# The last steps of the first attention group, reordered: transposes and copy of a pair of head columns, and the product of head 5

## The chip, the cores and the metric

The kernel runs on one core of a Trainium2 chip. The metric is device time in microseconds (us) of one execution; the time before is the median of five runs.

## The reference

Two operations follow one another. The first is causal attention over 4 batches, 8 heads, 768 positions and a head size of 64. Three heads (0, 2, 6) attend to all earlier positions; the other five see only the first 4 positions (sinks) and a window of the last 64. The second is a mixture of 4 experts on the 3072 x 512 attention output, all four applied to every token and weighted by normalised probabilities.

```python
scores = scale * np.matmul(q, k.transpose(0, 1, 3, 2))
causal = rel >= 0
stream_keep = causal & (is_sink | in_win)          # is_sink: key < 4; in_win: 0 <= rel < 64
mask = np.where(retr[0, :, 0, 0, None, None], full_mask, stream_mask)
...
a = a / (np.sum(a, axis=-1, keepdims=True) + 1e-09)
attn_out = np.matmul(a, v)
x = np.ascontiguousarray(attn_out.transpose(0, 2, 1, 3)).reshape(B * S, H * D)
p = domain_probs / (domain_probs.sum(-1, keepdims=True) + 1e-09)
for e in range(E):
    h = np.maximum(x @ w1[e], 0.0)
    out += p[:, e:e + 1] * (h @ w2[e])
```

## The kernel before

The 3072 tokens are cut into 8 groups of 384 (batch b, half c). Attention of a group leaves its result in a tile `xT` with the 512 model columns on partitions, as four columns of 128 that each hold two heads: `PLACE[h] = (h % 4, h // 4)`, so column 0 holds heads 0 and 4, column 1 heads 1 and 5, column 2 heads 2 and 6, column 3 heads 3 and 7. The MoE layers read `xT` as the moving operand. The first group's attention runs alone at the start, up to about 21 us; the attention of the other groups is mixed in small steps into the MoE work of earlier groups.

The order of instructions on each engine is written out by hand: an engine executes what the Python program issues for it in that order. The program is made of generators. Each `yield` hands over an estimate in ns, and the driver adds it to a running clock with `tick`. Work that should not stand too early in VectorE's queue is booked on a list, `behind`, with a due time of the clock plus `LAG` = 1300; `tick` issues from the front of the list what has come due:

```python
def later(op, g):
    behind.append((clock[0] + LAG, op, g))
def tick(ns):
    clock[0] += ns
    while behind and behind[0][0] <= clock[0]:
        behind.pop(0)[1]()
```

A retrieval head (`values_r`, L713) gives its values with tokens on partitions; the pair of heads 2 and 6 is normalised into `x_pair`, and `x_transposes(6)` turns it: three matmuls with the identity (L762) into a pV bank, and one VectorE copy (L766) into column 2 of `xT`. A streaming head (`values`, L785) has its values already turned. Its matmuls write a pO bank (heads of the upper half) or a pV bank. ScalarE takes the logarithm of the sums (L803) and the exponential of its negative (L813), and a booked `scale` multiplies on VectorE into the head's half of its `xT` column (L808). The loop over a streaming head's matmuls hands over inside only where the estimate passes 300 ns with matmuls left:

```python
ns += mm_ns(nq)
if ns > 300 and n < len(work) - 1:
    yield ns
    ns = 0
```

Here `mm_ns(cols)` is `cols / 2.4 + 2.5`. In the first group a streaming head has two score tiles with the parts 160 and 160, and 160 and 96 columns, so four value matmuls.

The first group ends with the values of heads 5 and 7 and the transposes of head 6's pair; then `tick(LAG)` and `small_things` (masks and the normalising of probabilities on VectorE). The driver's next work is `plain_steps` of expert 0. It opens four blocks of layer 1 (L1027), one PSUM bank each. For each block it issues the matmuls of columns 0, 2 and 1, block after block, and then column 3 of each, followed by the block's ReLU on ScalarE (L1040). Layer 2 is L1048. GpSimd issues the weight loads (L334, L340), and the loads of queries, keys and values.

Of the kernel before, what the change touches and what calls it, by code (L numbers as in the profile page):

```python
# [18 lines left out]
def kernel(  # L19
# [147 lines left out]
    def half(u):  # L167
        return slice(u * D, (u + 1) * D)
# [25 lines left out]
    def v_tile(b, c, h, t):  # L194

        if b:
            return v_tiles(b, c, h)[:, t, :]
        return v_tiles(b, t // TC, h)[:, t % TC, :]
# [115 lines left out]
    def sink_row(h):  # L314

        t = v_tiles(0, 0, h)
        nc.vector.tensor_copy(
            out=t[0:NS, :, own_v(h)],
            in_=v_s32[:, h : h + 1, :].to_broadcast([NS, TC, D]),
        )  # L320

    def sink_rows(b, c):
        if b:
            put_sinks(windows(vSf), v_sinks, c)
            return
        for t in range(TC):
            nc.sync.dma_start(
                out=vS[0:NS, c, t, :, :], in_=vS[R0 : R0 + NS, 0, 0, :, :]
            )
# [97 lines left out]
    def warm_up(ps, n, cols):  # L427
        for _ in range(n):
            nc.tensor.matmul(  # L429
                out=ps[:, 0:cols], lhsT=warm[:, 0:P], rhs=warm[:, 0:cols],  # L430
                start=True, stop=True,
            )
# [103 lines left out]
    def mm_ns(cols):  # L536
        return cols / 2.4 + 2.5

    def attention(b, c):
# [213 lines left out]
        def x_transposes(h):  # L753
            ct = PLACE[h][0]
            x = x_pair if ct else x_one
            r = slice(0, P) if ct else half(0)
            if h == 6:
                ps = pV.tile([P, 512], FP32, name="pV", bufs=2)
            else:
                ps = pO.tile([P, 512], FP32, name="pO", bufs=2)  # L760
            for j in range(3):
                nc.tensor.matmul(  # L762
                    out=ps[r, j * P : (j + 1) * P], lhsT=x[:, j, r], rhs=ident16,
                    start=True, stop=True,
                )
            nc.vector.tensor_copy(out=xT[g][r, ct, :], in_=ps[r, 0:CH])  # L766

        def values(h):
            if RETR[h]:
                yield from values_r(h)  # L770
                return
            ct, u = PLACE[h]
            if first and u == 1:
                ps = pO.tile([P, 512], FP32, name="pO", bufs=2)
            else:
                ps = pV.tile([P, 512], FP32, name="pV", bufs=2)
            if first:
                warm_up(ps, {3: 3, 4: 3, 5: 4, 7: 3}.get(h, 0), 256)
            work = []
            for es, parts in es_of[h]:  # L780
                for t, o, q0, nq in parts:
                    work.append((es, t, o, q0, nq))
            ns = 0
            for n, (es, t, o, q0, nq) in enumerate(work):
                nc.tensor.matmul(  # L785
                    out=ps[:, q0 : q0 + nq],
                    lhsT=v_tile(b, c, h, t),
                    rhs=es[:, o : o + nq],
                    start=(n == 0),
                    stop=(n == len(work) - 1),  # L790
                    skip_group_check=True,
# [6 lines that stand above are left out]
            r, o = half(u), half(1 - u)  # L798
            pair = first and h in (3, 4)
            if not pair or u == 0:  # L800
                rc_of[0] = att.tile([P, CH], FP32, name="rc", bufs=2)
            rc = rc_of[0]
            nc.scalar.activation(  # L803
                out=rc[r, :], in_=ps[o, 0:CH], func=AF.Ln, bias=eps[o, :]
            )

            def scale(r=r, ps=ps):
                nc.vector.tensor_tensor(  # L808
                    out=xT[g][r, ct, :], in0=ps[r, 0:CH], in1=rc[r, :], op=ALU.mult
                )  # L810

            if not pair:
                nc.scalar.activation(out=rc[r, :], in_=rc[r, :], func=AF.Exp, scale=-1.0)  # L813
                later(scale, g)
            elif u == 0:
                scale_of[0] = scale
            else:
                nc.scalar.activation(out=rc, in_=rc, func=AF.Exp, scale=-1.0)
                later(scale_of[0], g)
                later(scale, g)  # L820

            yield ns + (600.0 if g == 1 else 400.0)

        def both(a, bb):

            gens = [a, bb]
            while gens:
                for gg in list(gens):
                    try:
                        yield next(gg)  # L830
                    except StopIteration:
                        gens.remove(gg)
# [4 lines left out]
        if first:  # L837
            yield from transposes(0)
            yield from scores(0)
            sink_row(1)  # L840
            sink_row(3)
            yield from transposes(1)
            yield from scores(2)
            sink_row(4)
            sink_row(5)
            sink_row(7)
            yield from both(scores(1), values(0))
            yield from transposes(2)
            yield from both(scores(3), values(2))
            x_transposes(0)  # L850
            yield from scores(4)
            yield from transposes(3)
            yield from values(1)
            yield from both(scores(5), values(3))
            yield from both(scores(6), values(4))
            yield from both(scores(7), values(6))
            yield from values(5)
            yield from values(7)
            x_transposes(6)
            tick(LAG)  # L860
            small_things()
        else:
            order = (0, 2, 6, 1, 3, 5, 7, 4) if by_dma else (0, 2, 1, 3, 6, 5, 7, 4)
            more = divmod(g + 1, NCH) if g + 1 < G else None
            if not by_dma:
                sink_rows(b, c)

            def behind_values(h):
                if more and not RETR[h]:
                    load_v(*more, [h])  # L870
            if by_dma:
                keys_to_rows(b, c)
                yield 1500.0
            else:
                yield from transposes(0)
                yield from transposes(1)

            waiting = []
            for n, h in enumerate(order):
                v_steps, done = iter(()), None  # L880
                ahead = sum(len(score_tiles(x)) for x in (*waiting, h))
                if len(waiting) > 1 or (waiting and ahead > 6):
                    done = waiting.pop(0)
                    v_steps = values(done)
                for m, step in enumerate(both(scores(h), v_steps)):
                    yield step
                    if not by_dma and n == 1 and m == 1:
                        yield from transposes(3)
                if done is not None:
                    behind_values(done)  # L890
                waiting.append(h)
                if n < 3 and by_dma:
                    keys_to_windows(b, c, n)
                if n == 1 and by_dma:
                    sink_rows(b, c)
                if n == 3 and more and g > 1:
                    transpose_rows(*more)
                if not by_dma and n == 2:
                    yield from transposes(2)
            if more:  # L900
                if g == 1:
                    load_probs(pair0)
                    transpose_rows(*more)
            for h in waiting:
                yield from values(h)
                behind_values(h)

    def small_things():
        def to_mask(x, bias):
            nc.vector.tensor_scalar(  # L910
                out=x, in0=bias, scalar1=0.0, scalar2=None, op0=ALU.is_ge
            )

        to_mask(mC, bC)
        to_mask(mS[:, 0:3, :], bS)
        to_mask(mS[:, 3, :], bS[:, 2, :])
        normalise(probs, psums, p_sb)
# [21 lines left out]
    behind = []  # L939
# [3 lines left out]
# [7 lines that stand above are left out]
# [487 lines left out]
    for ns in attention(0, 0):  # L1437
        tick(ns)
# [108 lines left out]
```

The softmax here doesn't subtract the row's maximum and nothing guards it: scores larger than these inputs give would overflow.

## Time and profile before

| | us |
|---|---|
| median of five runs | 377.53 (377.0 to 377.95) |
| profiled execution, its own time | 377.52 |
| its span | 375.8 |
| TensorE busy | 368.1 (98%) |
| VectorE busy | 282.4 (75%) |
| ScalarE busy | 227.7 (61%) |
| granted TensorE clock | 0.999 |

The span runs from the first to the last instruction of the profiled execution; 1.7 us of its time lie outside. Engines are named PE (TensorE matmuls), PEld (its weight loads), DVE (VectorE), ACT (ScalarE), POOL (GpSimd) and SP (the sync engine). A line number such as L766 is that of the kernel. On a timeline, a row has its start, its length, engine, line, operation, what it writes and reads, the shape, the count of instructions merged into it, and in brackets how long its engine was idle before it and what released it.

### The profile page before, as it was taken

Reading aid. Unit: us, or ns where it says so; the run is one execution under the profiler, and the core shown is the slowest. Engines: PE = TensorE matmul, PEld = TensorE weight load, DVE = VectorE, ACT = ScalarE, POOL = GpSimd, SP = SyncE. Lnnn points to the kernel's source line nnn. Section 1 sums busy time; section 2 is a strip of 40 time slices with the busy share of each in tenths; the row PEclk is TensorE's granted clock in tenths of the full one; section 3 lists DMA queues with packets and bytes.
Section 4 is the critical chain, followed back from the end, with each engine's and each line's share of the span. In section 5 each row is a group of like instructions: output and inputs, shape, how many; then the busy total and the mean of one; then the engine's idle time right before and its main releaser. Section 6 shows DMA issues by size and latency. Waiting matters only on the chain.

```text
span 375.8 us, 10137 instructions
## 1 busy us (share of the span) xinstructions
PE 368.1 (98%) x4128; PEld 311.0 (83%) x4128; DVE 282.4 (75%) x620; ACT 227.7 (61%) x475; POOL 112.8 (30%) x155
## 2 busy tenths in 40 slices
PE   8889999999999999999999999999999999999996
PEld 4755466668998988999989898998899998999996
DVE  7774768697888679878758858967778868769572
ACT  3863478547785785765676955784777361450630
POOL 8933673693058038115601650320000000000000
PEclk9999999999999999999999999999999999999999
DMA  9999999999799579988904991951220300300101
GB/s 164 152 201 205 185 192 192 181 205 116 83 117 153 103 97 120 149 117 63 206 9 62 169 156 19 129 126 14 72 69 2 111 5 0 114 2 6 54 2 56
DMA packets 124771, 39.24 MB, mean 104 GB/s; under 512 B 113728, under 2 KB 118404, under 8 KB 124724
## 3 DMA queue, kind: packets, MB, share of 16 engines
q0 software_dynamic: 86848, 19.01, 58.5%
q1 hardware_dynamic: 36276, 19.18, 23.3%
q8 instruction: 32, 0.52, 0.6%
q10 hardware_dynamic: 1600, 0.39, 0.5%
q14 instruction: 15, 0.12, 0.1%
HBM read 44.89 MB, written 6.34 MB: 136 GB/s over the span
## 4 chain that ended last, share of the span: by engine, by line
PE 94%; DVE 3%; ACT 2%; issue 0%; ACTq 0%
PE pO L1290 31%; PE pA L1154 25%; PE pO L1183 9%; PE pA L1027 7%; PE pO L1048 7%; PE pA L659 5%; PE pV L713 2%; PE pV L785 2%; PE pA L1183 2%; PE pO L429 1%; PE pA L557 1%; ACT rc L803 1%; DVE xs L1112 1%; ACT es L677 1%; DVE kR L576 1%; PE pA L1380 0%
## 5 line engine op out<-in xcount | busy, mean ns | idle before, releaser
L1290 PEld LDWEIGHTS <-hA 128*128 128x128 f16 x1104 | 104.9, 98 | 12.3
L1154 PE MATMUL pA<-xs,w1sb 128*128 128x256 f16 x864 | 109.3, 272 | 0.0
L1154 PEld LDWEIGHTS <-w1sb 128*128 128x128 f16 x864 | 80.7, 98 | 8.5
L1163 ACT ACTIVATE hA<-pA 128x512 f16<-128x512 f32 x108 | 64.4, 597 | 35.2 <-PE pA L1154 32.9
L1290 PE MATMUL pO<-w2sb,hA 128*128 128x256 f16 x640 | 76.7, 272 | 0.0
L677 ACT ACTIVATE es<-pA 128x384 f16<-128x384 f32 (+2 forms) x122 | 59.2, 512 | 26.7 <-PE pA L659 22.9
L305 POOL DMA_DIRECT2D vS<-in_v_dram x30 | 29.6, 986 | 113.3 <-PE pV L785 110.1
L1290 PE MATMUL pO<-tsb,hA 128*128 128x256 f16 x464 | 56.7, 272 | 0.0
L1112 DVE TENSOR_TENSOR xs<-xT,pB 128x1024 f16<-128x1024 f16 (+1 forms) x52 | 49.5, 970 | 1.2 <-DMA xT<-x_pair 1.2
L967 DVE TENSOR_TENSOR hA<-hA 128x1024 f16<-128x1024 f16 x60 | 39.6, 684 | 0.4
L1040 ACT ACTIVATE hA<-pA 128x384 f16<-128x384 f32 (+1 forms) x64 | 22.2, 385 | 19.9 <-PE pA L1027 19.7
L1027 PE MATMUL pA<-xT,w1sb 128*128 128x384 f16 (+1 forms) x256 | 30.9, 273 | 1.3 <-DVE xT L766 0.8
L1048 PE MATMUL pO<-w2sb,hA 128*128 128x512 f16 x128 | 30.7, 379 | 0.0
L1310 ACT COPY s<-pO 128x256 f32<-128x256 f32 x31 | 11.5, 372 | 27.7 <-PE pO L1290 21.9
L1027 PEld LDWEIGHTS <-w1sb 128*128 128x128 f16 x256 | 19.3, 98 | 10.2 <-issue 1.9
L808 DVE TENSOR_TENSOR xT<-pV,rc 64x384 f16<-64x384 f32 x37 | 20.5, 555 | 9.0 <-ACT rc L813 6.6
L1183 PEld LDWEIGHTS <-w1sb 128*128 128x128 f16 x416 | 26.3, 98 | 1.1 <-issue 0.2
L803 ACT ACTIVATE rc<-pV,eps 64x384 f32<-64x384 f32 x37 | 21.3, 575 | 6.5 <-PE pV L785 5.9
L1199 DVE TENSOR_TENSOR hA<-pO,s 128x512 f16<-128x512 f32 x26 | 17.9, 687 | 9.3 <-PE pO L1183 6.7
L681 DVE TENSOR_TENSOR es<-es,mS 128x384 f16<-128x384 f16 (+1 forms) x40 | 13.7, 344 | 13.5 <-ACT es L677 13.4
L1193 ACT COPY s<-pO 128x512 f32<-128x512 f32 x39 | 22.5, 586 | 1.4 <-PE pO L1183 1.2
L1183 PE MATMUL pO<-xs,w1sb 128*128 128x128 f16 x312 | 23.3, 219 | 0.0
(144 smaller groups left out, 498.3 us busy)
## 6 DMA issues: line engine op xcount, KB each, us to landing
pB<-p_rows SPq DMA_DIRECT2D x10, 512.0 KB
out_dram<-o SPq DMA_DIRECT2D x19, 256.0 KB
w1sb<-in_moe_w_dram POOLq DMA_DIRECT2D x8, 512.0 KB, 9.2
w2sb<-in_moe_w_dram POOLq DMA_DIRECT2D x4, 1024.0 KB, 12.5
vS<-in_v_dram POOLq DMA_DIRECT2D x30, 112.0 KB, 4.2
k_rows<-in_k_dram POOLq DMA_DIRECT2D x18, 128.0 KB, 5.0
q<-in_q_dram POOLq DMA_DIRECT2D x18, 128.0 KB, 6.4
vR<-in_v_dram POOLq DMA_DIRECT2D x24, 48.0 KB, 5.7
```

The lines of the kernel that those rows point to most:

```text
L305: gp.dma_start(out=t[:, :, own_v(h)], in_=windows_of(v, b, h, c))
L677: nc.scalar.activation(out=es[:, 0:cols], in_=ps[:, 0:cols], func=AF.Exp, scale=SC)
L803: nc.scalar.activation(out=rc[r, :], in_=ps[o, 0:CH], func=AF.Ln, bias=eps[o, :])
L967: nc.vector.tensor_tensor(out=out, in0=a, in1=b, op=ALU.subtract)
L1027: nc.tensor.matmul(out=pss[ft][:, 0:cols_n], lhsT=w1sb[:, e * DMP + ct, ft * P : (ft + 1) * P], rhs=x[:, ct, :], start=(n == 0), stop=(n = ...
L1048: nc.tensor.matmul(out=ps_o, lhsT=hs[:, ft, j * P : (j + 1) * P], rhs=w2sb[:, e * FTP + ft, :], start=(ft == 0), stop=(ft == FTP - 1),)
L1112: nc.vector.tensor_tensor(out=o, in0=xin, in1=pb.to_broadcast([P, DMP, n, P]), op=ALU.mult)
L1154: nc.tensor.matmul(out=ps[:, f * PC : (f + 1) * PC], lhsT=w1sb[:, e * DMP + ct, (f0 + f) * P : (f0 + f + 1) * P], rhs=xs[:, ct, :], start= ...
L1163: nc.scalar.activation(out=blocks[:, b0 : b0 + 2, k0 : k0 + 2, :].rearrange("p t f x -> p f t x"), in_=ps.rearrange("p (f t x) -> p f t x" ...
L1183: nc.tensor.matmul(out=ps[:, f * P : (f + 1) * P], lhsT=w[:, ct, f * P : (f + 1) * P], rhs=a[:, ct, :], start=(first and f == 0 and ct == ...
L1193: nc.scalar.copy(out=kept[n], in_=ps)
L1290: nc.tensor.matmul(out=ps, lhsT=a[:, k, :], rhs=b(k), start=(first and k == 0), stop=(k == KT - 1), skip_group_check=not first,)
```

## The change

At the end of the first group, the last entry of `behind` is taken off once head 5's values have been issued; it is head 5's booked product. The generator of head 7's values is then advanced by one step, the transposes and the copy of the pair (`x_transposes(6)`) are issued, head 5's product is booked again with the clock of that moment, and the rest of head 7's generator follows. `tick(LAG)` and `small_things` come after that, as before.

```diff
             yield from both(scores(6), values(4))
             yield from both(scores(7), values(6))
             yield from values(5)
-            yield from values(7)
+            at_once = behind.pop()
+            v_steps = values(7)
+            yield next(v_steps)
             x_transposes(6)
+            later(*at_once[1:])
+            yield from v_steps
             tick(LAG)
             small_things()
```

## Prediction

> **What bounds the kernel now.** I read the page's busy times first, then the chain that ended last, then TensorE's waits after the first group, then the timelines of TensorE, VectorE and ScalarE around 20 us, where the change lies.
>
> From the page, busy time by engine and the shares of the chain:
>
> ```profile
> PE 368.1 (98%) x4128; PEld 311.0 (83%) x4128; DVE 282.4 (75%) x620; ACT 227.7 (61%) x475; POOL 112.8 (30%) x155
> PE 94%; DVE 3%; ACT 2%; issue 0%; ACTq 0%
> ```
>
> TensorE works for 368.1 of 375.8 us and is 94% of the chain. [...] its queue has hardly a hole: what delays it delays the end. Its waits after 20 us (engine and line, what it waited for: us in total, times, longest):
>
> ```profile
> PE pA L1027 <- DVE xT L766: 0.8, 1, 0.8
> PE pV L713 <- DVE es L681: 0.6, 1, 0.6
> PE pA L1027 <- DMA w1sb<-in_moe_w_dram: 0.4, 1, 0.4
> ```
>
> There are three, and two stand at the seam that the change touches, where the first MoE layer begins. The seam on the timelines (start us, us, engine, line, operation, count, idle before and its releaser); TensorE, then VectorE, then ScalarE. The last two TensorE rows are from narrow windows and share a matmul: it starts at 22.06:
>
> ```profile
> 19.66 0.41 PE L785 MATMUL pO<-es,vS 128*128 128x160 f16 x4
> 20.05 0.34 PE L762 MATMUL pV<-ident,x_pair 128*128 128x128 f16 x3
> 20.76 0.32 PE L1027 MATMUL pA<-xT,w1sb 128*128 128x384 f16 x1 [0.36 <-DMA w1sb<-in_moe_w_dram]
> 21.89 0.48 PE L1027 MATMUL pA<-xT,w1sb 128*128 128x384 f16 x2 [0.81 <-DVE xT L766]
> 22.06 0.65 PE L1027 MATMUL pA<-xT,w1sb 128*128 128x384 f16 x3
> ...
> 20.69 0.56 DVE L808 TENSOR_TENSOR xT<-pO,rc 64x384 f16<-64x384 f32 x1 [0.70 <-ACT rc L813]
> 21.28 0.56 DVE L766 CAST xT<-pV 128x384 f16<-128x384 f32 x1
> 21.87 0.56 DVE L808 TENSOR_TENSOR xT<-pO,rc 64x384 f16<-64x384 f32 x1
> 22.47 0.23 DVE L910 TENSOR_SCALAR mC<-early 128x256 f16<-128x256 f16 x1
> ...
> 19.53 0.57 ACT L803 ACTIVATE rc<-pO,eps 64x384 f32<-64x384 f32 x1 [0.30 <-PE pO L785]
> 20.14 0.52 ACT L813 ACTIVATE rc<-rc 64x384 f32<-64x384 f32 x1
> 20.68 0.57 ACT L803 ACTIVATE rc<-pO,eps 64x384 f32<-64x384 f32 x1
> 21.29 0.52 ACT L813 ACTIVATE rc<-rc 64x384 f32<-64x384 f32 x1
> ```
>
> VectorE does head 5's product (20.69), the pair's copy (21.28), head 7's product (21.87). Plain_steps takes its columns in the order 0, 2, 1, 3. Column 0 starts at 20.76; column 2, the pair, waits for the copy until 21.89; column 1, with head 5, follows at 22.06 without a wait, its product having ended at 21.25. Column 3, with head 7, is asked for only after twelve matmuls. ScalarE's reciprocal of head 7 ends at 21.29 + 0.52 = 21.81, and head 7's product can't start before it.
>
> [...] the matmuls behind column 2 of the first block, on columns ready long before, stood still until 21.89. [...] the copy's transposes ended at 20.05 + 0.34 = 20.39, yet it ran only after head 5's product. [...] Here that hop is 0.03 us from ScalarE to VectorE (20.66 to 20.69) and 0.05 from VectorE to TensorE (21.84 to 21.89).
>
> **The change, part by part.** It adds and removes no instruction and no DMA. What counts is the order in which instructions are issued.
>
> *The transposes.* Read literally, they should fall within head 7's value matmuls. They don't. The generator of head 7 hands over inside its loop only once its estimate exceeds 300 ns with matmuls left. In this group a streaming head has four matmuls of 160, 160, 160 and 96 columns; at columns / 2.4 + 2.5 they come to 69, 138, 207 and 250, so it never does. Its first yield is its last: all four matmuls, both ScalarE operations and the booking of head 7's product have been issued. TensorE's order is as before, value matmuls at 19.66 and transposes at 20.05. Cost 0, and ScalarE's order is unchanged too.
>
> *The copy.* Head 5's product has been taken off the list, so the copy is first on VectorE. It waits for the transposes, 20.39; with a hop of 0.03 it runs 20.42 to 20.98. No row shows it so early; whether 0.02 sooner or 0.5 later doesn't matter, for it isn't what ends last below. Column 2 of the first block could then start at 20.98 + 0.05 = 21.03, 0.86 us earlier.
>
> *Head 5's product.* It is booked again only after the transposes, and head 7's was booked inside the step before. The list is served from its front: at tick(LAG) **head 7's product comes out first, head 5's second**. Head 7's product waits for ScalarE until 21.81, so it starts at 21.84 and ends at 22.40. VectorE's starts in this row are 0.59 apart: head 5's product runs 22.43 to 22.99, although its inputs were there at 20.66. It has gone from first to third. VectorE stands idle from 20.98 to 21.84.
>
> *TensorE behind it.* The third matmul of the first block, column 1, needs head 5's product: 22.99 + 0.05 = 23.04, where it started at 22.06. **That is 0.98 us later.** Behind it in program order stand the other columns of that block, the next three blocks, and the whole kernel. Only one matmul, column 2's, moves in front of the wait; it was the one just ahead of column 1 before, so the displacement of everything from column 1 on is 0.98. Column 3 asks for head 7's product (22.40) ten matmuls after that and waits for nothing.
>
> *What hides nothing of it.* After this seam TensorE's waits name one stall, 0.57 us before 43.59 (L713, for a mask product on VectorE). Followed back, VectorE there runs without a hole from 40.20, when it was released by TensorE's own transposes at 39.80; it moves along. From then on the longer pieces of the chain are TensorE's, apart from two of 1.13 us on VectorE near 205, which follow earlier TensorE work. No transfer is awaited after 20.76.
>
> *What moves beside it, at no cost.* The masks and the normalising of the probabilities begin behind the third product, 23.03 for 22.47: 0.56 later, with SP's store of the probability rows (27.02) behind them and SP's four copies of sinks after that. VectorE is idle 2.12 us before its next use at 29.11 (from its timeline), and the first reader of the masks is past 43. Without that cover it would be 0.56, still less than TensorE's own shift. GpSimd's loads up to 30 us wait for earlier loads, not for this. The two pO banks are read until 22.99; TensorE next writes one past 27.
>
> *The clock.* The third matmul waits from about 21.35 to 23.04, 1.7 us; the longest hole so far was 1.03 (before 18.35), and the granted clock reads 1.00 in every slice. [...] I take 0[...].
>
> Sum: +0.98 on the profiled execution's 377.52 us (span 375.8, so 1.7 outside it) gives 378.50; the median shown, 377.53, is the same within 0.01, so **378.5 us**.
>
> **The rivals.** *Head 5's product directly behind the copy*, the reading that the words suggest. Then it runs 21.01 to 21.57, column 1 starts at 21.62, 0.44 earlier than 22.06, and head 7's product at 21.84 is in time: 377.1, not slower. It decides on one point: whether head 5's product leaves the list before head 7's. It is no loss as long as that product ends by 22.01. For it: the four value matmuls could be handed over in two pieces if the estimate passed 300. Against it: the sum is 250.
>
> *The delay is partly swallowed.* If the stall before 43.59 is held by something that doesn't move, up to 0.57 comes back: +0.41, 377.9. Against it is the chain from 39.80 just given.
>
> *The clock drops.* [...] Against it is the hole's length; for it, that only two of this layer's matmuls run between 20.4 and 23.0.
>
> *The change doesn't do what it says*: as to the transposes that holds already, and is in the main case.
>
> **How the numbers follow.** Main case 0.80, 378.5 with its own spread of 0.3; swallowed 0.08, 377.9; clock 0.06[...]; the other order 0.06, 377.1. A measurement of this kernel can tell about 0.2%, 0.75 us, from no change: slower means over 378.28. The main case lies 0.22 above that, and some 0.07 of its chance falls below; with the swallowed case and most of the other order, same is 0.15, faster 0.02, slower 0.83. The range, 377.9 to 379.2, holds the main case, half the swallowed one and a clock loss of up to 0.7; about 0.16 is left out.
>
> **What the next profile would show.** VectorE at the seam: the copy near 20.42, then an idle of about 0.85 released by ScalarE L813, then two L808 products near 21.84 and 22.43. TensorE: one L1027 at 20.76, one near 21.03, then a wait of about 1.7 us for xT of L808, and the rest from 23.04. ScalarE's four rows as they were. If one product stands between copy and 21.6, the order is the rival's. If the seam is as said and the end isn't about 1 us later, look at 43: the L713 stall would be shorter. A granted clock under 1.0 in the slices up to 30 us would be the clock's.

## The result, and the profile after

| | before | changed |
|---|---|---|
| median, us | 377.5 (41 executions) | 379.7 (22 executions) |
| lowest to highest | 377.0 to 378.53 | 377.87 to 380.52 |
| profiled execution, its span | 377.52, 375.8 | 379.7, 378.0 |
| mean granted TensorE clock there | 0.999 | 0.995 |

The ratio is 1.005, with a 95% interval of 1.0041 to 1.0059. That is slower, as forecast, but by 2.2 us where 1.0 was forecast, and above the range. The clock records fall into two groups: 15 of the 22 executions stand at 0.994 or 0.995 and took 379.38 to 380.52, the other 7 at 0.999 or 1.0 and took 377.87 to 379.31. Of these seven, five lie between 377.87 and 378.31, and two, at 379.30 and 379.31, close to the first group; they were not profiled.

The seam (the place where the first group's attention ends and the first layer begins) comes first: the timelines of the changed kernel around 20 us, TensorE, VectorE and ScalarE (start us, length us, engine, line, operation, count; idle before and its releaser in brackets). Lines behind the change are four higher: L1027 is now L1031, L1048 is L1052.

```profile
20.06 0.34 PE L762 MATMUL pV<-ident,x_pair 128*128 128x128 f16 x3
20.77 0.60 PE L1031 MATMUL pA<-xT,w1sb 128*128 128x384 f16 x2 [0.37 <-DMA w1sb<-in_moe_w_dram]
22.93 6.71 PE L1031 MATMUL pA<-xT,w1sb 128*128 128x384 f16 x30 [1.56 <-DVE xT L808]
...
20.44 0.56 DVE L766 CAST xT<-pV 128x384 f16<-128x384 f32 x1 [0.44 <-PE pV L762]
21.85 1.03 DVE L808 TENSOR_TENSOR xT<-pO,rc 64x384 f16<-64x384 f32 x2 [0.85 <-ACT rc L813]
22.91 0.23 DVE L914 TENSOR_SCALAR mC<-early 128x256 f16<-128x256 f16 x1
...
21.30 0.52 ACT L813 ACTIVATE rc<-rc 64x384 f32<-64x384 f32 x1
```

The order is the one read from the code. The transposes are where they were. The copy is first on VectorE, at 20.44. VectorE then idles 0.85 us for head 7's reciprocal, and both products follow in one row of two, head 7's and then head 5's. TensorE does two matmuls of the layer, columns 0 and 2, and stands 1.56 us for head 5's product. Column 1 starts at 22.93 for 22.06, 0.87 later.

The rest is in the same TensorE row: thirty matmuls take 6.71 us, where thirty-one took 5.45 in the kernel before:

```profile
21.89 5.45 PE L1027 MATMUL pA<-xT,w1sb 128*128 128x384 f16 x31 [0.81 <-DVE xT L766]
```

The clock row of the profile's 40 slices and the stretches after 22 us of the changed kernel show why (columns: stretch, its length, busy us and count of TensorE, its weight loads, VectorE, ScalarE and GpSimd, the granted clock, DMA share, GB/s):

```profile
PEclk9989999999999999999999999999999999999999
```

```profile
core 0: us, PE busy (x) PEld busy (x) DVE busy (x) ACT busy (x) POOL busy (x), PEclk, DMA share, GB/s
22.00:23.00 1.00, 0.07 (x1) 0.06 (x1) 0.97 (x3) 0.00 (x0) 0.43 (x1) 1.00 1.27 212
23.00:24.00 1.00, 1.00 (x6) 0.52 (x6) 0.90 (x7) 0.00 (x0) 0.00 (x0) 0.76 1.24 208
24.00:25.00 1.00, 1.00 (x5) 0.50 (x4) 0.97 (x6) 0.00 (x0) 0.00 (x0) 0.50 1.15 180
25.00:26.00 1.00, 1.00 (x5) 0.50 (x4) 0.97 (x2) 0.00 (x0) 0.00 (x0) 0.50 1.15 209
26.00:27.00 1.00, 1.00 (x5) 0.48 (x4) 0.97 (x4) 0.89 (x3) 0.30 (x2) 0.53 1.09 201
27.00:28.00 1.00, 1.00 (x8) 0.59 (x6) 0.43 (x2) 1.00 (x3) 0.77 (x1) 1.00 1.13 213
```

In the row of slices only the third, 18.9 to 28.4 us, is under 9. In the stretches the busy share is 1.00 from 23 us on and tells nothing apart; the count does: five matmuls touch a microsecond in which the clock reads 0.50, eight the one after it. From one matmul's start to the next it is 0.32 us there, and 0.16 after it. The clock reads 0.50 from 23.52 (0.76 in the second stretch is 0.48 us at 0.50) to 26.93 (0.53 in the fifth is 0.94 us at 0.50), 3.41 us in all. This is called the drop from here on.

Setting each matmul against the same one of the kernel before gives where the time went. Column 1 of the first block is 0.87 later; the sixteenth matmul, the last of the four blocks' column 3, 2.34; the seventeenth 2.25, since in the kernel before it started some 0.25 us late, by the kernel's order because a ReLU had yet to free its bank, and now it comes too late to wait that long; and from the first layer-2 matmuls of expert 1 (38.84 in the kernel before) to the end 2.21, with no further step. So 0.87 is the wait and about 1.4 the clock; 0.1 comes back at those layer-2 matmuls.

### The profile page after: what moved, and what is told of

Read it like the earlier page. It is cut to its first block, busy times and chain, and to the rows that moved or that the text cites. A ratio compares the mean times of both kernels' runs of the same rounds, so it can differ in the third digit from the quotient of the medians.

```text
span 378.0 us, 10136 instructions
## 1 busy us (share of the span) xinstructions
PE 369.6 (98%) x4128; PEld 311.5 (82%) x4128; DVE 281.6 (75%) x620; ACT 227.8 (60%) x475; POOL 112.8 (30%) x155
## 4 chain that ended last, share of the span: by engine, by line
PE 94%; DVE 3%; ACT 2%; issue 0%; ACTq 0%
PE pO L1294 31%; PE pA L1158 25%; PE pO L1187 9%; PE pA L1031 8%; PE pO L1052 7%; PE pA L659 5%; PE pV L713 2%; PE pV L785 2%; PE pA L1187 2%; PE pO L429 1%; PE pA L557 1%; ACT rc L803 1%; DVE xs L1116 1%; ACT es L677 1%; DVE xT L808 1%; DVE kR L576 1%
## 5 line engine op out<-in xcount | busy, mean ns | idle before, releaser
L1031 PE MATMUL pA<-xT,w1sb 128*128 128x384 f16 (+1 forms) x256 | 32.6, 281 | 1.9 <-DVE xT L808 1.6
L1052 PE MATMUL pO<-w2sb,hA 128*128 128x512 f16 x128 | 30.7, 379 | 0.0
L1031 PEld LDWEIGHTS <-w1sb 128*128 128x128 f16 x256 | 19.9, 100 | 11.9 <-issue 4.2
L659 PE MATMUL pA<-qT,kR 128*128 128x384 f16 (+2 forms) x120 | 22.9, 278 | 0.5 <-DVE kR L576 0.4
```

Of the source, the lines that this page charges most:

```text
L659: nc.tensor.matmul(out=ps[:, o : o + nq], lhsT=key_tile(b, c, h, t), rhs=qTs[b, c][:, hp, q0 : q0 + nq], start=(n == 0 or not first), stop ...
L1031: nc.tensor.matmul(out=pss[ft][:, 0:cols_n], lhsT=w1sb[:, e * DMP + ct, ft * P : (ft + 1) * P], rhs=x[:, ct, :], start=(n == 0), stop=(n = ...
L1052: nc.tensor.matmul(out=ps_o, lhsT=hs[:, ft, j * P : (j + 1) * P], rhs=w2sb[:, e * FTP + ft, :], start=(ft == 0), stop=(ft == FTP - 1),)
```

## The experiments

The theory: the loss has two parts. Head 5's product comes third on VectorE, and TensorE waits 0.87 us longer. And TensorE then does so little around that wait that its clock drops, in some executions and not in others. The rivals: the drop comes from the reordering itself, from one long unbroken hole (a time in which TensorE stands still), or by chance; the wait is partly given back.

**Head 5's product right behind the copy.**

```diff
-            later(*at_once[1:])
+            behind.insert(0, (clock[0] + LAG, *at_once[1:]))
```

> The changed kernel with head 5's product put at the front of the list, so that it follows the copy and precedes head 7's product. Theory (the loss comes from head 5's product standing third): it runs near 21.0 to 21.6, column 1 starts near 21.6 where it started at 22.06 in the kernel before, the clock stays at 1.00, 377.05 us (-0.45 against before). Rival (moving the copy ahead costs by itself, whatever follows): as the changed kernel, 379.7.

Measured: 377.25 us over 13 executions, ratio 0.9996 (0.9987 to 1.0005), clock 0.999 or 1.0 in all. TensorE's timeline at the seam, and its waits (what it waited for: us in total, times, longest):

```profile
20.54 0.60 PE L1031 MATMUL pA<-xT,w1sb 128*128 128x384 f16 x2 [0.37 <-DMA w1sb<-in_moe_w_dram]
21.41 5.29 PE L1031 MATMUL pA<-xT,w1sb 128*128 128x384 f16 x30 [0.27 <-DVE xT L808]
```

```profile
PE pV L713 <- DVE es L681: 0.6, 1, 0.6
PE pO L1052 <- DMA w2sb<-in_moe_w_dram: 0.4, 1, 0.4
PE pA L1031 <- DMA w1sb<-in_moe_w_dram: 0.4, 1, 0.4
PE pA L1031 <- DVE xT L808: 0.3, 1, 0.3
```

The whole loss goes with the place of head 5's product; that the copy is ahead costs nothing. This execution runs 0.22 us ahead already before the seam. Past it, column 1 is 0.65 ahead, so the seam itself gives 0.42. A wait of 0.4 for expert 1's second weights, which no row of the kernel before names, takes that back: at the matmul that stands at 38.84 in the kernel before, the lead is 0.18.

**The hole filled with dummy matmuls**, once into a bank taken for it, once into the bank of the pair's transposes.

```diff
             for ft in pss:
                 for n in range(DMP - 1):
+                    if nt0 == 0 and e == 0 and ft == 0 and n == 2:
+                        warm_up(bank_for_it, 12, 256)   # pV.tile(...), or the transposes' bank
                     layer1(ft, n)
```

> The changed kernel with twelve dummy matmuls of 256 columns on zeros into a spare pV bank, issued between column 2 and column 1 of the first block, about 1.3 us within the 1.7 us that TensorE waits there. Theory (the wait costs 0.87 us by itself, and the rest of the 2.2 us is a clock that drops because TensorE stood still): no slice under 1.0, column 1 near 22.93 as in the changed kernel, 378.4 us. Rival (with a full clock half of the delay comes back, as some full-clock executions of the changed kernel at 377.87 suggest): 377.9. Rival (the clock doesn't drop for want of matmuls): 379.7 with the same drop.

> As e2_busy_hole, with the twelve dummy matmuls written into the pV bank that the pair's transposes used, so that no bank is taken and the alternation of the two pV banks in all later groups stays as in the changed kernel. e2 came to 378.88, with 0.5 us lost at 248 us behind a transposing load of x_pair that landed late. Theory (the added bank changed later groups, and the wait at the seam alone costs 0.87): no wait of TensorE near 248, clock at 1.0 throughout, 378.3 to 378.4. Rival (the late x_pair load comes with any delay of this size and has nothing to do with the bank): 378.9 again with the same wait.

Measured: 378.88 us (5 executions; 1.0038, 1.0026 to 1.005) and 378.65 (10; 1.0031, 1.0021 to 1.0042). The clock is at 0.999 or 1.0 in all fifteen, where it was at 0.994 or 0.995 in 15 of 22 of the changed kernel: with the hole filled, the drop doesn't come. TensorE and its waits in the second of the two, and VectorE's wait before its products of MoE inputs, there and in the kernel before:

```profile
21.22 1.47 PE L429 MATMUL pV<-early 128*128 128x256 f16 x12
22.95 2.27 PE L1033 MATMUL pA<-xT,w1sb 128*128 128x384 f16 x13 [0.26 <-DVE xT L810]
```

```profile
PE pO L1191 <- DVE xs L973: 0.4, 1, 0.4
```

```profile
DVE xs L1120 <- DMA xT<-x_pair: 2.4, 1, 2.4
```

```profile
DVE xs L1112 <- DMA xT<-x_pair: 1.2, 1, 1.2
```

Column 1 is displaced by 0.88 in both, and 0.1 of it is given back at expert 1's second weights. Then both profiles lose some 0.53 near 248 us, where a product of MoE inputs waits longer for a transposing load of `x_pair`. The bank isn't the cause, for the second version, which takes none, loses it too. Nor need the whole kernel be late for it: one of the two profiles of the last version below, which runs 0.8 ahead there, loses 0.66 at the same matmul, after a wait of VectorE put down to another DMA (`out_dram`), and the other profile of that version doesn't. So it differs between executions of one kernel; it doesn't stand in the profiles of the kernel before or of the changed one. Both medians lie 0.25 to 0.5 above the 378.4 that the wait alone gives; whether these late loads make all of that isn't settled.

**Column 3 ahead of column 1, and a longer hole.**

```diff
-            cts = (0, 2, 1, 3)
+            cts = (0, 2, 3, 1) if nt0 == 0 and e == 0 and f0 == 0 else (0, 2, 1, 3)
```

> The changed kernel, but the first four blocks take column 3 (head 7's product) ahead of column 1 (head 5's). The third matmul then waits for the product that is ready 0.47 us sooner: from about 21.2 to 22.45, a hole of 1.25 us for 1.72. Theory (delay from the product that is waited for, and a drop that depends on the length of the hole): the delay against before is 0.4, 377.9 us if the clock holds, and the drop is rarer than in the changed kernel. Rival (the drop comes from the reordered VectorE queue and not from the length of the hole): a drop as often as in the changed kernel, about 379.3.

```diff
-            later(*at_once[1:])
             yield from v_steps
             tick(LAG)
+            small_masks()     # the part of small_things that makes the masks
+            at_once[1]()
             small_things()
```

> The changed kernel with the three masks ahead of head 5's product on VectorE, which makes TensorE's wait about 0.5 us longer, to about 23.4. Theory (length of the hole decides): the delay is 1.35 and the drop comes in every execution, 380.2 to 380.5 us. Rival (a drop once in a while, by chance): as the changed kernel plus 0.5, with executions at full clock as often as there.

The waits of TensorE for the product, first with column 3 ahead, then with the masks ahead:

```profile
PE pA L1031 <- DVE xT L808: 1.1, 1, 1.1
```

```profile
PE pA L1034 <- DVE xT L808: 2.1, 1, 2.1
```

With column 3 ahead, 377.62 us (13 executions; 1.0003, 0.9995 to 1.0011) and no drop: the VectorE queue is that of the changed kernel, instruction for instruction, and the rival that blames the reordering falls. The third matmul is 0.22 later than in the kernel before, in an execution that came to the seam 0.18 ahead: a displacement of 0.40, as expected. With the masks ahead, 379.54 (6 executions; 1.0072, 1.0045 to 1.0099), and only three of six dropped, at 380.5 to 381.7; the other three took 378.49 to 378.55. The expectation of a drop every time was wrong. The profile is of one without: a wait of 2.08 us, 0.5 longer than the changed kernel's, and a mean clock of 1.0. Why it was spared isn't shown. The distance of 2.0 to 3.1 between the two groups is more than 3.41 us at 0.50, as in the profile of the changed kernel, can cost, an estimated 1.7. The spared execution came to the seam 0.71 ahead of the kernel before (its transposes start at 19.34 for 20.05); how much that explains stays open, for none with a drop was profiled.

**The old order with less work around the hole.** The kernel before, without the seven dummy matmuls ahead of the value matmuls of heads 5 and 7.

```diff
-                warm_up(ps, {3: 3, 4: 3, 5: 4, 7: 3}.get(h, 0), 256)
+                warm_up(ps, {3: 3, 4: 3}.get(h, 0), 256)
```

> The kernel before, with its old order on VectorE, without the seven dummy matmuls of 256 columns ahead of the value matmuls of heads 5 and 7 (four and three, 0.77 us of TensorE work between 18.6 and 19.7). Nothing that column 1 waits for becomes later, and the hole before the second column stays at about 0.8 us. Theory [...]: [...] the clock drops in a good part of the executions, those 1.2 to 1.6 us longer than the others, 378.5 to 379 against 377.5. Rival (one unbroken hole of over 1.7 us decides): no drop, 377.3 to 377.6.

Measured: 377.8 us (14 executions), ratio 1.0014 (1.0004 to 1.0023). Five of the fourteen have clocks of 0.991 to 0.995 and took 377.75 to 379.53, the nine others 377.39 to 378.02. Of the kernel before's executions that ran beside these experiments, 2 of 115 have a clock under 0.999 (0.991 and 0.996, at 381.37 and 382.92); why is not known. TensorE's timeline in one of the nine, and one of its waits:

```profile
18.67 0.41 PE L785 MATMUL pO<-es,vS 128*128 128x160 f16 x4
19.37 0.41 PE L785 MATMUL pO<-es,vS 128*128 128x160 f16 x4 [0.28 <-ACT es L677]
20.07 0.34 PE L762 MATMUL pV<-ident,x_pair 128*128 128x128 f16 x3 [0.29 <-DVE x_pair L742]
20.46 0.32 PE L1027 MATMUL pA<-xT,w1sb 128*128 128x384 f16 x1
21.64 5.45 PE L1027 MATMUL pA<-xT,w1sb 128*128 128x384 f16 x31 [0.85 <-DVE xT L766]
```

```profile
PE pO L1048 <- DMA w2sb<-in_moe_w_dram: 0.7, 1, 0.7
```

No hole here is longer than about 1 us (the longest, 1.03, ends at 18.37), and yet five other executions have a lower clock, where 2 of 115 of the kernel before have one. As far as this profile stands for them, it takes no hole longer than those that the kernel before has (1.03 before 18.35); seven matmuls less, and the short holes left in their place, are enough. The price was lower than expected, about 0.6 us between the medians of the two groups. The wait of 0.7 for expert 1's second weights could hide that much of a drop; but no execution with a drop was profiled here, so that, and where in them the clock was low, stay open.

**The changed kernel again, and with three dummies.**

> The changed kernel as it is, for its spread: theory [...]: two groups of executions, those whose clock record stays at 0.999 or 1.0 at 377.9 to 378.4 (a wait longer by 0.87, and some tenths less at the start), those at 0.995 near 379.8, some two thirds to four fifths of them. Rival (one broad group, the clock's record being incidental): times between 378.5 and 379.5 as often as outside.

> The changed kernel, one more profile, for one execution with a full clock: theory, if the clock stays at 1.0 [...] the displacement stays at 0.87 from column 1 on. [...] Rival (the drop follows the hole at a fixed distance[...]): a drop beginning at 23.0 to 23.5 in every execution.

Twelve of 17 executions dropped (379.63 to 380.73), five did not (377.57 to 378.11); between 378.11 and 379.63 there is nothing in these seventeen. The median is 379.71. A further execution of the changed kernel kept its clock, at 377.88. Its TensorE timeline at the seam and two stretches:

```profile
22.54 5.29 PE L1031 MATMUL pA<-xT,w1sb 128*128 128x384 f16 x30 [1.57 <-DVE xT L808]
```

```profile
20.00:24.00 4.00, 2.07 (x12) 1.10 (x13) 2.98 (x14) 1.36 (x3) 1.69 (x3) 1.00 1.23 204
24.00:28.00 4.00, 3.91 (x24) 2.24 (x23) 2.96 (x7) 3.14 (x8) 1.06 (x2) 1.00 1.14 202
```

The wait is again 1.57 us, the clock reads 1.00 in both stretches, and thirty matmuls take 5.29. So a wait of this length comes with the drop in one execution and without it in another; what sets the two apart isn't shown. Their starts differ too. The first transposes, in the first profile and in this one:

```profile
4.71 1.51 PE L557 MATMUL pA<-early,hA 128*128 128x128 f32 x6
```

```profile
4.74 0.84 PE L557 MATMUL pA<-early,hA 128*128 128x128 f32 x6
```

In the kernel before's profile the six take 1.51 us as well. This execution is 0.39 ahead of that profile on reaching the seam, leaves it 0.48 behind, a displacement of 0.87 as in the others, and ends 0.39 behind. So this execution, spared by the drop, also started early, and the distance between the two groups is larger than the drop alone.

The three dummies, in the bank of the transposes:

```diff
-                        warm_up(same_bank[0], 12, 256)
+                        warm_up(same_bank[0], 3, 256)
```

> As e9_busy_hole_same_bank with three dummy matmuls instead of twelve, 0.33 us of work in the hole[...]. Column 1 starts when it does in the changed kernel. Theory [...]: [...] the clock drops in clearly fewer executions than the 27 of 39 of the changed kernel, a fifth or less. Rival (the drop is set off by the wait itself): as often as there, with a median of 379.7.

Measured: 378.11 us (15 executions; 1.0022, 1.001 to 1.0033). Two of fifteen dropped, at 379.69 and 379.75, against 27 of 40 of the changed kernel. TensorE at the seam, in a profile without the drop:

```profile
20.82 0.49 PE L429 MATMUL pV<-early 128*128 128x256 f16 x3
22.55 5.29 PE L1033 MATMUL pA<-xT,w1sb 128*128 128x384 f16 x30 [1.24 <-DVE xT L810]
```

Three matmuls on zeros, a row of 0.49 us, take away most drops and 1.6 us of the median; the wait for the product stays, 1.24 us of it unfilled.

**Head 5's product right behind the copy once more, and the load that took the gain.** The kernel is that of the first experiment, with one change more:

```diff
-    load_w2(1)
+    load_w2(1, 2)      # the same load in two halves, one behind the other
```

> Head 5's product right behind the copy, as in e1_product5_next, and expert 1's second weights loaded in two halves instead of one load. In e1 column 1 starts 0.42 us sooner, and 0.4 of it is lost again at the first layer-2 matmul of expert 1, which waits for that load. Theory (that load swallows the gain): its first half lands sooner, the wait of L1052 is gone, 377.0 us or less. Rival (the gain is lost elsewhere, or the halves land no sooner): as e1, 377.25.

> e8_order_and_w2_halves once more, for its interval: theory (the seam is 0.42 us earlier and nothing later takes it back) 377.0 us against 377.45 before, a ratio near 0.9988. Rival (its median of 377.06 was a favourable draw): 377.3 or more, no different from the kernel before.

Measured: 377.06 us (14 executions; 0.9997, 0.9982 to 1.0012) and 377.21 (21; 0.9991, 0.9977 to 1.0005), beside 377.46 and 377.44 of the kernel before. TensorE's waits after 17 us in the first:

```profile
PE pV L715 <- ACT es L679: 1.0, 1, 1.0
PE pV L715 <- DVE es L683: 0.6, 1, 0.6
PE pA L1033 <- DVE xT L768: 0.3, 1, 0.3
PE pA L1033 <- DVE xT L810: 0.3, 1, 0.3
```

The wait for expert 1's second weights is gone, column 1 is 0.40 ahead, and the end 0.50. The medians are 0.2 to 0.4 better than the kernel before, but both intervals hold 1: this version is well ahead of the changed kernel, but a gain over the kernel before isn't shown.

## Why the prediction was right or wrong

*The order on the engines, and the direction: right.* The transposes are unmoved, the copy is first (20.44; forecast 20.42), VectorE is idle for 0.85, and head 7's product comes before head 5's. With that order alone changed, the loss is gone.

*The wait: the right mechanism, 0.98 where 0.87 was measured.* The mis-sized term is the start of head 5's product, 22.43. I took VectorE's spacing of 0.59 from a row in which each operation was of another kind or waited for another engine. Two products back to back take 1.03 us, not 1.15: the second starts about 0.48 after the first and ends at 22.88, where I had 22.99.

*What hides it: nearly right.* "No transfer is awaited after 20.76" was wrong by 0.1: in the profiles of all versions that came late to expert 1's second weights and met no longer wait there, the displacement shrank by 0.1, so the kernel before had waited that long for them, too little for a row. The stall at L713 moved along as argued. The wait for those weights matters more for a gain: in the first experiment it took 0.46 of a lead of 0.65.

*The clock: the step that failed.* "I take 0" went by the length of the one hole and gave the clock a chance of 0.06. That a hole of this length leaves the clock alone was an estimate that no trace showed. The profile of the changed kernel has the clock at 0.50 for 3.41 us, from 23.52, 0.59 us after the wait had ended. Nor do the runs bear out that the length of one hole decides: the kernel without the seven dummies had lower clocks in 5 of 14 executions, though its profile shows no hole of more than about 1 us; the three dummies nearly stopped the drop, 2 of 15, with a hole of some 1.2 us left; and with a wait of 2.1 us 3 of 6 were spared. What they do show is that the matmuls around the seam matter: the drop came in 5 of 14 when seven were taken away there, with no product later on VectorE, and in none of 15 when twelve were put in, with the same product late. How little is too little, and why some executions are spared, isn't shown. The point named for this case, that only two of this layer's matmuls run between 20.4 and 23.0, was the better one. The term that I put at 0 measured 1.4 in the profiled execution, and the range had room for 0.7.

*The numbers.* An execution without the drop and without an early start should take about 378.3 (377.52, and 0.87 less 0.1), near the forecast 378.5; none of that kind was profiled, and the executions without the drop took 377.57 to 379.31. Two in three had the drop, so the median went to 379.7. The swallowed case was wrong as to its place: 0.1 came back, at expert 1's second weights and not at L713. The other order was priced at 377.1, and 377.25 was measured when it was made.

## What to carry to other kernels

Follow a booked or deferred operation to the point where it leaves its list: moving one instruction ahead can push another, which is awaited sooner, behind one that isn't ready. Where TensorE is the bound, add up its work around a wait and not only the length of the single hole; here the lower clock after it cost more than the wait itself, 1.4 us for 0.87, in some executions and not in others. A gain ahead of a load that lands no sooner can be lost there, here 0.46 of a lead of 0.65, while nearly all of a loss stays, here all but 0.1 of 2.3.

## What the runs showed of the hardware that was not expected

- In the profile of the changed kernel the granted clock read 0.50 from 23.52 to 26.93 us, 3.41 us, and TensorE's matmuls of 384 columns started 0.32 us apart for 0.16; the wait ahead of it, 1.56 us, had ended at 22.93.
- Executions with a clock of 0.991 to 0.996, and in brackets TensorE's wait for a product or the copy at the seam in a profile: 27 of 40 of the changed kernel (1.56 and 1.57 us in two), 3 of 6 with the masks ahead (2.08), 5 of 14 in the old order without the seven dummies (0.85), 2 of 15 with three dummies in the wait (1.24 left), none of 13 with column 3 ahead (1.09), none of 15 with twelve dummies (at most 0.26 left) and none of 13 with head 5's product right behind the copy (0.27). The order isn't that of the waits.
- Three dummy matmuls on zeros, a row of 0.49 us, took these from 27 of 40 executions to 2 of 15.
- Executions of one kernel differ at the start: the first six transposes of the changed kernel took 1.51 us in one profile and 0.84 us in another, and the second came to the seam 0.40 us earlier. Why isn't shown.
